# One attention and two-layer kernel: attention steps begun earlier, rounding split over two slots, all masks through ScalarE and GpSimd

## The chip, the core and the metric

The kernel runs on one core of a Trainium2 chip. The metric is the device time of one execution in microseconds (us), of which 0.2% (some 2 us) is about what a measurement of this kernel can tell from no change.

## What is computed

A gated linear attention over 768 positions, for 4 batches of 8 heads with head size 48, then two feed-forward layers over the 3072 resulting rows of 384 numbers:

```python
f = 1.0 / (1.0 + np.exp(-f_logit))
for t in range(S):
    state = f[:, :, t, :, None] * state + np.einsum('bhd,bhe->bhde', k[:, :, t], v[:, :, t])
    y[:, :, t] = np.einsum('bhd,bhde->bhe', q[:, :, t], state)
x = (x @ w_a) * (x @ w_b) @ w_out      # d_ff 1536
h = x @ w_in                           # d_ff 2048
out = (h - np.tanh(h)) @ w_out2
```

All inputs are float32. A product of two float32 matrices is made of three TensorE passes on rounded high halves and on low halves (`mm_split`: high by high, high by low, low by high), so each operand is first split: ScalarE copies it with rounding (the high half), then VectorE or GpSimd subtracts (the low half).

## The kernel before

**Attention steps.** Positions are cut in chunks of 64, and the four batches in two halves, which makes 24 steps; a step (`attn_step`, L289) handles one chunk of one half of the batches. It is a generator that yields between phases, and a phase has a letter:

- F: ScalarE's Sigmoid (L299). P: VectorE's scan PRE (L301). R: PMS, a reciprocal, and the reverse scan R (L304 to L306). K: VectorE's KH, RA and RB (L313 to L315). V: ScalarE copies the state into VS_A and VS_B (L318, L319).
- S: TensorE's scores sc from KH, RA and RB, and the transposes pk of KH (L327 to L331). M: the mask on sc, into RA and RB, and ScalarE's copy KTS of pk (L336 to L344). In steps 0 to 7 (`i < PSEL`) the mask is a ScalarE copy and a GpSimd select; from step 8 on VectorE multiplies by a tile of ones and zeros (L343).
- U: TensorE's uu from KTS, VectorE's T (L359), GpSimd's new state ST (L362). Y: TensorE's yy (L369). E: yy is split in high and low halves, of the tile y and of the tile x (ScalarE L383, VectorE L384). D: DMAs on ScalarE's and SyncE's queues move y into x (L390).

PSUM banks for sc, pk, the two uu and yy rotate: over two banks while block 0 runs, over three later (`att_bank`, `rot`).

**The first layer.** The rows of x are six blocks of 512, four steps each. `moe1` (L482) goes through block after block, and in each through 12 tiles m of d_ff. A tile has three parts, called slots here: nine matmuls a (then ScalarE's copy asb, L497), nine matmuls b (then VectorE's product gf, ScalarE's gh and the low half gl, L502 to L509), and nine matmuls y of the tile before (`y_group`). So a block has 36 slots. Steps 0 to 3 run ahead of everything, in the order of the string SEQ, in which x stands for a dummy matmul (warm) and c for one weight conversion; this is called the prologue. The steps of block j + 1 run in the slots of block j: phase p of its step si stands at slot 9 si + OFF[p] - LEAD of block j. Phases at negative slots fall into the block before, and for block 1 into SEQ.

**Weights.** The first layer's 36 weight tiles (w_a, w_b, w_o of each m) and the second layer's 32 come as compressed integers. A conversion (`w_tick`) is three VectorE instructions (L125 to L127, called a conversion below), a ScalarE copy w (L137) and a subtraction on GpSimd or, for the second layer, on VectorE (L139). In block 0 each slot makes one conversion of the first layer; in blocks 1 to 4 those of the second layer come at two slots of nine (`CONV`). Two conversions stand in SEQ, so in block 0 a conversion is made two ahead of the part that needs it.

At the start of blocks 1 to 5, in slot 2, the last y of the block before is finished, split by ScalarE (oh, L471) and VectorE (ol, L472) and written out (`store_x2`). The second layer comes after block 5, without attention.

Every engine works its instructions in the order in which this code emits them.

Of the kernel before, what the change touches and what calls it, by code (L numbers as in the profile page):

```python
# [9 lines left out]
F32 = mybir.dt.float32  # L10
# [3 lines left out]
ACTF = mybir.ActivationFunctionType  # L14
ALU = mybir.AluOpType
# [3 lines left out]
CH = 64  # L19
# [9 lines left out]
def tile_kernel(ctx: ExitStack, tc: tile.TileContext, q, k, v, f, w_a, w_b, w_out, w_in, w_out2, l_fkq, l_tv, l_v, l_w1, l_w2, out):  # L29
    nc = tc.nc  # L30
# [9 lines left out]
    U = 2 * NJ  # L40
# [8 lines left out]
    first = [sum(blocks[:j]) for j in range(NBLK)]  # L49
    block_of = [j for j, n in enumerate(blocks) for _ in range(n)]  # L50
    PRO = blocks[0]
    SLOTS = 3 * MF
    LEAD = 3
    PHASES = "FPRKVSMUYED"
    OFF = (0, 0, 1, 3, 4, 5, 5, 7, 8, 8, 9)
    CONV = (2, 6)
    PSEL = first[2]
    SEQ = ("lf0 lk0 lf1 lt0 lk1 lv0 lf2 lt1 lv1 lk2 w lf3 lt2 lv2 lk3 w lt3 lv3 w x x x x F0 P0 F1 R0 K0 x x lf4 lk4 x V0 S0 P1 M0 F2 "
           "R1 K1 U0 Y0 lt4 lv4 x V1 S1 P2 E0 F3 M1 R2 K2 x U1 Y1 x V2 S2 P3 E1 M2 R3 K3 x U2 Y2 x V3 S3 c E2 M3 c U3 x Y3 x F4 E3 P4")
    TW = 528  # L60

    const = ctx.enter_context(tc.tile_pool(name="const", bufs=1))
# [3 lines left out]
    stage = wctx.enter_context(tc.tile_pool(name="stage", bufs=2))  # L66

    ident = const.tile([128, 128], F32, name="ident")
    mask = const.tile([128, CH], F32, name="mask")
    D1 = const.tile([128, NS], F32, name="D1")  # L70
    PMS = const.tile([128, NSTEP, U], F32, name="PMS")
    okf = const.tile([1, 1], I32, name="okf")
# [70 lines left out]
    def w_spill():  # L143
        name, m, wt = spilled.pop(0)
        nc.sync.dma_start(out=wsp[2 * m + "ip".index(name)], in_=wt.bitcast(F32))
# [13 lines left out]
    def att_bank(name):  # L159
        rot["att"] = (rot["att"] + 1) % rot["n"]  # L160
        return bank(rot["att"], name)
# [5 lines left out]
    with tc.manual_schedule(), ExitStack() as p1:  # L167
# [81 lines left out]
        def load_v(i):  # L249
            w = w_of(i)  # L250
            for ab, (vs, r0) in enumerate(((w.VS_A, 64), (w.VS_B, 0))):
                nc.sync.dma_start(out=vs[r0:r0 + 64], in_=l_v[i, ab])
# [20 lines left out]
        for s_ in VX:  # L273
            for t in s_:
                nc.gpsimd.memset(t, 0.0)
        nc.gpsimd.memset(mask, 1.0)
        for r0 in (0, 64):
            nc.gpsimd.affine_select(
                out=mask[r0:r0 + 64], in_=mask[r0:r0 + 64], compare_op=ALU.is_ge, fill=0.0,
                base=0, pattern=[[1, CH]], channel_multiplier=-1,  # L280
            )

        X = {}
        Y3 = {}

# [3 lines left out]
        def attn_step(i):  # L289
            c, hb = divmod(i, 2)  # L290
# [34 lines left out]
            sc = att_bank("sc").rearrange("p (u s) -> p u s", s=CH)  # L325
# [6 lines left out]
                    pk[:, 128 * j:128 * (j + 1)], KH[:, 2 * j:2 * j + 2, :].rearrange("p u s -> p (u s)"), ident)  # L332
            yield
            for r_, rows in ((RA, slice(64, 128)), (RB, slice(0, 64))):
                if i < PSEL:
                    nc.scalar.activation(r_[rows], sc[rows], ACTF.Copy)  # L336
                    nc.gpsimd.affine_select(
                        out=r_[rows], in_=r_[rows], compare_op=ALU.is_ge, fill=0.0,
                        base=0, pattern=[[0, U], [1, CH]], channel_multiplier=-1,
                    )  # L340
                else:
                    m3 = mask.unsqueeze(1)
                    nc.vector.tensor_tensor(r_[rows], sc[rows], m3[rows].to_broadcast([64, U, CH]), ALU.mult)  # L343
            nc.scalar.activation(KTS, pk, ACTF.Copy)  # L344
            yield
            uus = [att_bank(f"uu{bl}").rearrange("p (u s) -> p u s", s=CH) for bl in range(2)]
# [32 lines left out]
            evac = [(xh[:, :, si], xl[:, :, si], yy[:, 0:U - 2].rearrange("p (j b) s -> p j (b s)", b=2))]  # L379
            if not direct:  # L380
                evac.insert(0, (Y3[jb][:, 0, si], Y3[jb][:, 1, si], yy[:, U - 2:U].rearrange("p b s -> p (b s)")))
            for dh, dl, src in evac:
                nc.scalar.activation(dh, src, ACTF.Copy)  # L383
                nc.vector.tensor_tensor(dl, src, dh.bitcast(F32), ALU.subtract)  # L384
            yield
            if si == ns - 1 and not direct:
                for kt in range(KT):
                    for hf, q_ in enumerate((nc.scalar, nc.sync)):
                        r, p0 = 64 * hf + 16 * kt, 48 + 64 * hf
                        q_.dma_start(  # L390
                            out=X[jb][p0:p0 + 16, :, kt, 0:ns].bitcast(F32),
                            in_=Y3[jb][r:r + 16, :, 0:ns].bitcast(F32))
# [9 lines left out]
        def flag(pr):  # L402
            nc.tensor.transpose(pr[0:1, 0:128], ru, ident)
            nc.vector.tensor_reduce(r2, pr[0:1, 0:128], mybir.AxisListType.X, ALU.min)
            nc.vector.tensor_scalar(okf, r2, 0.5, None, ALU.is_ge)

        gens = {i: attn_step(i) for i in range(NSTEP)}
        pulses = []
        for jb in range(1, NBLK):
            for si in range(blocks[jb]):  # L410
                for p, o in enumerate(OFF):
                    at = (9 * si + o) * SLOTS // (9 * blocks[jb]) - LEAD
                    pulses.append((SLOTS * (jb - 1) + at, first[jb] + si, p))
# [4 lines left out]
        def pulse(i, p):  # L418
            assert phase[i] == p
            phase[i] += 1  # L420
            if i >= PRO and p == 0 and i + 1 < NSTEP:
                load_t(i + 1, slice(0, 3))
                load_tv(i + 1)
            next(gens[i], None)
            if i >= PRO and PHASES[p] == "Y" and i + 1 < NSTEP:
                load_v(i + 1)
# [11 lines left out]
        def w_tick(upto):  # L438
            while nconv[0] < upto and (loaded or half):
                if loaded:  # L440
                    half.append(w_start(loaded.pop(0)))
                    w_fetch()
                if len(half) > 1 or not loaded or half[0][0] in "abo":
                    w_finish(half.pop(0))
                nconv[0] += 1
# [70 lines left out]
        for it in SEQ.split():  # L516
# [6 lines left out]
            elif it[0] == "l":  # L523
                i = int(it[2])
# [6 lines left out]
            else:  # L531
                i, p = int(it[1]), PHASES.index(it[0])
                if i >= PRO:
                    pulses.pop(0)
                pulse(i, p)
        for i in range(PRO):
            pulse(i, len(PHASES) - 1)
        npro = nconv[0]
# [13 lines left out]
        for g, jb in enumerate(moe1(None)):  # L552
# [3 lines left out]
            else:  # L556
                if g == SLOTS:
                    rot.update(n=3, conv=None)
                if spilled:
                    w_spill()  # L560
                if (g + LEAD) % (SLOTS // 4) in CONV and jb < NBLK - 1 or (jb == NBLK - 1 and slot == 0):
                    w_tick(min(nconv[0] + 1, NW2 + 1))
            while pulses and pulses[0][0] <= g:
                _, i, p = pulses.pop(0)
# [247 lines left out]
```

## Time and profile before

| what | value |
|---|---|
| median of 3 runs | 1009.82 us (1008.72 to 1010.71) |
| profiled execution, own time | 1008.59 us |
| its span | 1006.8 us |
| TensorE (PE) busy | 962.3 us, 96% of the span |
| VectorE (DVE) busy | 653.6 us, 65% |
| ScalarE (ACT) busy | 461.2 us, 46% |
| GpSimd (POOL) busy | 105.5 us, 10% |

The profiled execution's own time is 1.8 us over its span and 1.2 us under the median. The first a matmul starts at 39.3 us. Block 0 runs from there to about 158 us, blocks 1 to 4 to 528 us, block 5 to 603 us, the second layer to the end. A share of the whole span hides these stages, so the rows below are taken by stage.

### The profile page before, as it was taken

The numbers are of one execution on the slowest core, as the hardware profiler recorded it, in microseconds if no ns is written. First come the engines' busy times: TensorE is split into PE (matmuls) and PEld (weight loads), VectorE is DVE, ScalarE is ACT, GpSimd is POOL, SyncE is SP. The second block draws the span as 40 slices with busy tenths as digits, with TensorE's granted clock in tenths as the row PEclk, the third lists the DMA queues.
The fourth block names the chain that finished last, engine by engine and source line by source line (L and its number), as shares of the span: only waits on it lengthen the run. The fifth ranks groups of instructions, "written<-read, shape, count | busy, mean of one in ns | idle before, by whom it ended". The sixth has DMA issues, their size and how long they took to land.

```text
span 1006.8 us, 15823 instructions
## 1 busy us (share of the span) xinstructions
PE 962.3 (96%) x6151; PEld 769.9 (76%) x6151; DVE 653.6 (65%) x1077; ACT 461.2 (46%) x893; POOL 105.5 (10%) x115
## 2 busy tenths in 40 slices
PE   7788888999999999999999999999999999999997
PEld 4566666888788777878888888888888888888885
DVE  8788786666776676666663228666666666666663
ACT  4344442333333333333332127666666666666663
POOL 6455551000000000100000000000000000000000
PEclk9999998999999999999999999999999999999999
DMA  9365554444644453364428652010100100200000
GB/s 278 90 171 165 149 137 128 118 128 121 192 117 119 112 183 118 109 183 123 114 63 329 191 161 104 1 75 20 63 32 1 64 32 1 94 1 1 32 1 35
DMA packets 41170, 104.52 MB, mean 104 GB/s; under 512 B 5600, under 2 KB 8672, under 8 KB 41088
## 3 DMA queue, kind: packets, MB, share of 16 engines
q1 hardware_dynamic: 40368, 102.45, 34.0%
q10 hardware_dynamic: 720, 0.98, 0.5%
q8 instruction: 50, 0.82, 0.4%
q14 instruction: 32, 0.26, 0.1%
HBM read 74.71 MB, written 26.74 MB: 101 GB/s over the span
## 4 chain that ended last, share of the span: by engine, by line
PE 81%; DVE 11%; ACT 3%; issue 3%; DMA 2%; SPq 0%; POOL 0%; DVEq 0%; ACTq 0%
PE o L165 20%; PE h L165 20%; PE y L165 12%; PE a L165 12%; PE b L165 11%; PE yy L369 2%; DVE cv L126 2%; DVE cv L125 1%; DVE wc L127 1%; PE sc L327 1%; DVE R L306 1%; PE uu L351 1%; PE pk L331 1%; DMA x<-y 1%; DVE RB L315 1%
## 5 line engine op out<-in xcount | busy, mean ns | idle before, releaser
L165 PE MATMUL h<-x,w_i 128*128 128x512 f32 x864 | 213.0, 391 | 0.0
L165 PE MATMUL o<-gh,w_p 128*128 128x512 f32 x576 | 194.7, 393 | 0.0
L165 PEld LDWEIGHTS h<-x,w_i 128*128 128x128 f32 x864 | 162.2, 188 | 36.4
L165 PE MATMUL a<-x,w_a 128*128 128x512 f32 x648 | 166.1, 400 | 3.6 <-DMA x<-y 3.2
L165 PE MATMUL b<-x,w_b 128*128 128x512 f32 x648 | 163.4, 397 | 6.1 <-ACT w_b L137 5.0
L165 PE MATMUL y<-gh,w_o 128*128 128x512 f32 x432 | 151.1, 404 | 4.4 <-ACT w_o L137 3.3
L165 PEld LDWEIGHTS b<-x,w_b 128*128 128x128 f32 x648 | 123.2, 191 | 34.9 <-ACT w_b L137 6.3
L165 PEld LDWEIGHTS a<-x,w_a 128*128 128x128 f32 x648 | 118.6, 189 | 30.8 <-DMA x<-y 2.7
L105 DVE SCALAR_TENSOR_TENSOR xu<-u,h 128x512 f32<-128x512 f32 x96 | 66.0, 687 | 111.5 <-ACT u L102 111.3
L165 PEld LDWEIGHTS o<-gh,w_p 128*128 128x128 f32 x576 | 108.2, 188 | 24.7
L503 ACT ACTIVATE gh<-gf 128x512 fp32r<-128x512 f32 x72 | 45.5, 632 | 165.2 <-DVE gf L502 161.1
L102 ACT ACTIVATE u<-h 128x512 f32<-128x512 f32 x96 | 57.4, 598 | 132.8 <-PE h L165 132.1
L165 PE MATMUL o<-gl,w_p 128*128 128x512 f32 x288 | 113.1, 393 | 0.0
L165 PEld LDWEIGHTS y<-gh,w_o 128*128 128x128 f32 x432 | 82.0, 190 | 25.9 <-ACT w_o L137 4.9
L497 ACT ACTIVATE asb<-a 128x512 f32<-128x512 f32 x72 | 43.0, 597 | 100.0 <-PE a L165 99.4
L165 PE MATMUL y<-gl,w_o 128*128 128x512 f32 x216 | 85.8, 397 | 0.0
L502 DVE TENSOR_TENSOR gf<-asb,b 128x512 f32<-128x512 f32 x72 | 49.0, 681 | 54.2 <-PE b L165 49.6
L107 DVE SCALAR_TENSOR_TENSOR v<-v,v 128x512 f32<-128x512 f32 x96 | 66.5, 693 | 10.3 <-ACT gh L583 0.5
L106 DVE SCALAR_TENSOR_TENSOR v<-v,xu 128x512 f32<-128x512 f32 x96 | 66.5, 692 | 10.4 <-ACT v L103 0.5
L103 ACT ACTIVATE v<-u,bias 128x512 f32<-128x512 f32 x96 | 69.6, 725 | 3.1
L104 ACT ACTIVATE v<-u,bias 128x512 f32<-128x512 f32 x96 | 68.1, 710 | 0.7 <-DVE gl L584 0.7
L584 DVE TENSOR_TENSOR gl<-v,gh 128x512 fp32r<-128x512 f32 x96 | 65.8, 685 | 0.2 <-ACT gh L583 0.2
(100 smaller groups left out, 1105.1 us busy)
## 6 DMA issues: line engine op xcount, KB each, us to landing
wst<-in_l_w_dram SPq DMA_DIRECT2D x68, 384.0 KB, 3.3
wsp<-wst SPq DMA_DIRECT2D x32, 384.0 KB, 2.3
T<-in_l_fkq_dram SPq DMA_DIRECT2D x38, 288.0 KB, 5.1
x<-xs SPq DMA_DIRECT2D x12, 768.0 KB, 5.7
w_i<-wsp SPq DMA_DIRECT2D x16, 384.0 KB, 3.5
w_p<-wsp SPq DMA_DIRECT2D x16, 384.0 KB, 3.5
TV<-in_l_tv_dram SPq DMA_DIRECT2D x24, 192.0 KB, 5.1
xs<-oh SPq DMA_DIRECT2D x18, 256.0 KB, 2.2
```

What stands on the lines that cost most here:

```text
L102: nc.scalar.activation(u, h, ACTF.Square, accum_out=total)
L103: nc.scalar.activation(v1, u, ACTF.Square, bias=bias1)
L104: nc.scalar.activation(v2, u, ACTF.Square, bias=bias2)
L105: nc.vector.scalar_tensor_tensor(xu, u, Q4, h, ALU.mult, ALU.mult)
L106: nc.vector.scalar_tensor_tensor(v1, v1, Q_Y1, xu, ALU.add, ALU.mult)
L107: nc.vector.scalar_tensor_tensor(v2, v2, Q_Y2, v1, ALU.add, ALU.mult)
L126: nc.vector.scalar_tensor_tensor(t, hi, -1073741824, t, ALU.bitwise_and, ALU.bitwise_or)
L165: nc.tensor.matmul(dst, l_, r_, start=(first and i == 0), stop=(last and i == 2))
L497: nc.scalar.activation(asb, pb, ACTF.Copy)
L502: nc.vector.tensor_tensor(gf, asb, pab[1], ALU.mult)
L503: nc.scalar.activation(gh, gf, ACTF.Copy)
L584: nc.vector.tensor_tensor(gl, g, gh.bitcast(F32), ALU.subtract)
```

## The change

Five things change. The new phase L takes the VectorE half of E into a slot of its own: E now makes both ScalarE copies, L both subtractions. P gets a slot of its own after F; with both, the offsets of a step run from 0 to 11 instead of 0 to 9. LEAD is 6 instead of 3, so against before F stands three slots earlier, P to E two, the subtractions and D one; `CONV` follows. All steps mask with ScalarE's copy and GpSimd's select, and the tile of ones and zeros goes. SEQ has three conversions instead of two, three more dummy matmuls, and the phases R4, K4 and V4 of block 1's first step, which stood in block 0.

```diff
-    LEAD = 3
-    PHASES = "FPRKVSMUYED"
-    OFF = (0, 0, 1, 3, 4, 5, 5, 7, 8, 8, 9)
-    CONV = (2, 6)
-    PSEL = first[2]
+    LEAD = 6
+    PHASES = "FPRKVSMUYELD"
+    OFF = (0, 1, 2, 4, 5, 6, 6, 8, 9, 9, 10, 11)
+    CONV = (3, 7)
...
-           "R1 K1 U0 Y0 lt4 lv4 x V1 S1 P2 E0 F3 M1 R2 K2 x U1 Y1 x V2 S2 P3 E1 M2 R3 K3 x U2 Y2 x V3 S3 c E2 M3 c U3 x Y3 x F4 E3 P4")
+           "R1 K1 U0 Y0 lt4 lv4 x V1 S1 P2 E0 F3 M1 R2 L0 K2 x U1 Y1 x V2 S2 P3 E1 M2 L1 R3 K3 x U2 Y2 x V3 S3 x x E2 M3 c L2 F4 c P4 "
+           "x x U3 x Y3 x E3 L3 R4 c K4 V4")
...
-                if i < PSEL:
-                    nc.scalar.activation(r_[rows], sc[rows], ACTF.Copy)
-                    nc.gpsimd.affine_select(
-                        out=r_[rows], in_=r_[rows], compare_op=ALU.is_ge, fill=0.0,
-                        base=0, pattern=[[0, U], [1, CH]], channel_multiplier=-1,
-                    )
-                else:
-                    m3 = mask.unsqueeze(1)
-                    nc.vector.tensor_tensor(r_[rows], sc[rows], m3[rows].to_broadcast([64, U, CH]), ALU.mult)
+                nc.scalar.activation(r_[rows], sc[rows], ACTF.Copy)
+                nc.gpsimd.affine_select(
+                    out=r_[rows], in_=r_[rows], compare_op=ALU.is_ge, fill=0.0,
+                    base=0, pattern=[[0, U], [1, CH]], channel_multiplier=-1,
+                )
...
             for dh, dl, src in evac:
                 nc.scalar.activation(dh, src, ACTF.Copy)
+            yield
+            for dh, dl, src in evac:
                 nc.vector.tensor_tensor(dl, src, dh.bitcast(F32), ALU.subtract)
             yield
```

ScalarE at the end of the prologue: w_a and w_b are the copies of the first two conversions, x the high half of a step (E), RA, RB and KTS those of M3, F the Sigmoid of step 4, asb the first of block 0. Before:

```order
L137 ACTIVATE w_a_584<-wc 128x384
L383 ACTIVATE x<-yy 128x3x128
L336 ACTIVATE RA<-sc 64x512
L336 ACTIVATE RB<-sc 64x512
L344 ACTIVATE KTS<-pk 128x512
L137 ACTIVATE w_b_601<-wc 128x384
L299 ACTIVATE F<-T_181 128x8x64
L383 ACTIVATE x<-yy 128x3x128
L497 ACTIVATE asb<-a 128x512
```

And now:

```order
L371 ACTIVATE x<-yy 128x3x128
L327 ACTIVATE RA<-sc 64x512
L327 ACTIVATE RB<-sc 64x512
L332 ACTIVATE KTS<-pk 128x512
L136 ACTIVATE w_a_590<-wc 128x384
L291 ACTIVATE F<-T_180 128x8x64
L136 ACTIVATE w_b_605<-wc 128x384
L371 ACTIVATE x<-yy 128x3x128
L136 ACTIVATE w_a_675<-wc 128x384
L310 ACTIVATE VS_A<-ST_130 64x8x48
L311 ACTIVATE VS_B<-ST_130 64x8x48
L487 ACTIVATE asb<-a 128x512
```

M3's three copies now stand ahead of the copy of the first conversion instead of behind it.

VectorE in block 0, around the low halves of step 4 and the scan PRE of step 5 (cv and wc are a conversion, gf the product of a tile). Before:

```order
L127 SCALAR_TENSOR_TENSOR wc<-wst,cv 128x384
L384 TENSOR_TENSOR y_865<-yy,y_865 128x128
L384 TENSOR_TENSOR x<-yy,x 128x3x128
L125 TENSOR_SCALAR cv<-wst 128x384
L126 SCALAR_TENSOR_TENSOR cv<-wst,cv 128x384
L127 SCALAR_TENSOR_TENSOR wc<-wst,cv 128x384
L301 SCALAR_TENSOR_TENSOR PRE<-F,D_68 128x520
L502 TENSOR_TENSOR gf<-asb,b 128x512
```

And now:

```order
L126 SCALAR_TENSOR_TENSOR wc<-wst,cv 128x384
L374 TENSOR_TENSOR y_831<-yy,y_831 128x128
L374 TENSOR_TENSOR x<-yy,x 128x3x128
L293 SCALAR_TENSOR_TENSOR PRE<-F,D_67 128x520
L124 TENSOR_SCALAR cv<-wst 128x384
L125 SCALAR_TENSOR_TENSOR cv<-wst,cv 128x384
L126 SCALAR_TENSOR_TENSOR wc<-wst,cv 128x384
```

The subtractions and the scan now stand in one slot, one conversion behind the ScalarE copies y and x and the Sigmoid that they need.

ScalarE at the start of block 1, from the first asb on. Before:

```order
L497 ACTIVATE asb<-a 128x512
L503 ACTIVATE gh<-gf 128x512
L318 ACTIVATE VS_A<-ST_131 64x8x48
L319 ACTIVATE VS_B<-ST_131 64x8x48
L471 ACTIVATE oh<-y_823 128x512
L471 ACTIVATE oh<-y_824 128x512
L471 ACTIVATE oh<-y_825 128x512
L344 ACTIVATE KTS<-pk 128x512
```

And now:

```order
L487 ACTIVATE asb<-a 128x512
L327 ACTIVATE RA<-sc 64x512
L327 ACTIVATE RB<-sc 64x512
L332 ACTIVATE KTS<-pk 128x512
L493 ACTIVATE gh<-gf 128x512
L461 ACTIVATE oh<-y_867 128x512
L461 ACTIVATE oh<-y_868 128x512
L461 ACTIVATE oh<-y_869 128x512
```

KTS moves from behind the three copies oh of the block's end to ahead of them, and the two mask copies stand beside it; on VectorE the two mask products go.

## Rows read from the trace of the kernel before

**Rows 1.** Windows by stage: length; busy PE, PEld, DVE, ACT, POOL; clock; DMA; GB/s.
```profile
39.30:160.30 121.00, 101.14 (x725) 75.16 (x726) 99.48 (x166) 46.56 (x90) 60.73 (x58) 0.95 0.55 146
160.30:528.00 367.70, 361.40 (x2898) 289.86 (x2897) 246.28 (x439) 124.35 (x234) 21.61 (x16) 0.99 0.45 129
528.00:603.00 75.00, 75.00 (x329) 61.26 (x328) 20.23 (x31) 17.83 (x30) 0.00 (x0) 1.00 0.67 223
```

**Rows 2.** Timeline, end of the prologue: start, us, instruction [idle before <-releaser].
```profile
32.00 0.52 ACT L137 ACTIVATE w_a<-wc 128x384 fp32r<-128x384 f32 x1 [3.99 <-DVE wc L127]
32.93 0.59 ACT L336 ACTIVATE RA<-sc 64x512 f32<-64x512 f32 x1
...
34.67 0.27 PE L351 MATMUL uu<-TV,KTS 64*64 64x48 f32 x4 [3.21 <-ACT KTS L344]
...
39.31 0.50 PE L165 MATMUL a<-x,w_a 128*128 128x512 f32 x1 [0.26 <-ACT x L383]
```

**Rows 3.** Windows behind two long waits of PE, columns as in rows 1.
```profile
36.00:38.50 2.50, 2.50 (x48) 2.50 (x48) 0.14 (x1) 0.22 (x1) 1.65 (x2) 0.50 1.00 288
158.20:164.70 6.50, 6.03 (x14) 4.79 (x15) 3.10 (x4) 0.60 (x1) 0.86 (x1) 0.50 0.02 4
```

**Rows 4.** Timeline of DVE: K's last instruction in steps 4, 5 and 7.
```profile
46.20 0.69 DVE L315 TENSOR_TENSOR RB<-T,PRE 64x512 f32<-64x512 f32 x1
...
75.10 1.39 DVE L315 TENSOR_TENSOR RB<-T,PRE 64x512 f32<-64x512 f32 x1
...
134.62 1.39 DVE L315 TENSOR_TENSOR RB<-T,PRE 64x512 f32<-64x512 f32 x1
```

**Rows 5.** Waits of DVE, 40 to 158 us: us in total, times, longest.
```profile
DVE PRE L301 <- ACT F L299: 6.4, 4, 2.9
...
DVE y L384 <- ACT y L383: 3.0, 4, 0.8
DVE x L384 <- ACT x L383: 2.2, 4, 0.6
```

**Rows 6.** Timeline of DVE, block 0: two conversions' starts, P, and R.
```profile
47.53 0.56 DVE L125 TENSOR_SCALAR cv<-wst 128x384 int32<-128x384 int32 x1
...
49.37 0.56 DVE L125 TENSOR_SCALAR cv<-wst 128x384 int32<-128x384 int32 x1
...
93.37 1.57 DVE L301 TENSOR_TENSOR_SCAN PRE<-F,D 128x520 f32<-128x520 f32 x1 [1.18 <-ACT F L299]
...
97.08 0.55 DVE L304 TENSOR_SCALAR PMS<-PRE 128x8 f32<-128x8 f32 x1
...
97.90 2.00 DVE L306 TENSOR_TENSOR_SCAN R<-F,D 128x520 f32<-128x520 f32 x1
```

**Rows 7.** Timeline, ACT's queue, SP's queue and PE, from block 0 into block 1.
```profile
151.81 0.71 ACTq L390 DMA_DIRECT2D x<-y  x1
...
152.09 0.58 SPq L247 DMA_DIRECT2D T<-in_l_fkq_dram  x1
...
154.96 0.93 PE L165 MATMUL a<-x,w_a 128*128 128x512 f32 x3 [1.39 <-DMA x<-y]
158.67 1.65 PE L165 MATMUL a<-x,w_a 128*128 128x512 f32 x3 [0.53 <-DMA x<-y]
160.12 4.04 PE L165 MATMUL b<-x,w_b 128*128 128x512 f32 x9
```

**Rows 8.** Waits of PE, 160 to 604 us: us in total, times, longest.
```profile
PE uu L351 <- DVE RB L343: 4.6, 3, 1.5
PE uu L351 <- ACT KTS L344: 1.0, 3, 0.4
PE sc L328 <- DVE RB L315: 0.7, 3, 0.3
```

**Rows 9.** Groups by shape: count, busy us, mean ns: VectorE's mask, GpSimd's select.
```profile
L343 DVE TENSOR_TENSOR RA<-sc,mask 64x512 f32<-64x512 f32 x16 | 11.1, 695 | 1.9 <-PE sc L328 0.9
...
L337 POOL TENSOR_SCALAR_AFFINE_SELECT RB<-RB 64x512 f32<-64x512 f32 x8 | 6.7, 838 | 0.5
```

More of the change, by code (lines that the diff above doesn't have):

```diff
@@ L68, in tile_kernel @@
     ident = const.tile([128, 128], F32, name="ident")
-    mask = const.tile([128, CH], F32, name="mask")
     D1 = const.tile([128, NS], F32, name="D1")
@@ L275, in tile_kernel @@
                 nc.gpsimd.memset(t, 0.0)
-        nc.gpsimd.memset(mask, 1.0)
-        for r0 in (0, 64):
-            nc.gpsimd.affine_select(
-                out=mask[r0:r0 + 64], in_=mask[r0:r0 + 64], compare_op=ALU.is_ge, fill=0.0,
-                base=0, pattern=[[1, CH]], channel_multiplier=-1,
-            )
         X = {}
@@ L334, in attn_step @@
             for r_, rows in ((RA, slice(64, 128)), (RB, slice(0, 64))):
-                if i < PSEL:
-                    nc.scalar.activation(r_[rows], sc[rows], ACTF.Copy)
-                    nc.gpsimd.affine_select(
-                        out=r_[rows], in_=r_[rows], compare_op=ALU.is_ge, fill=0.0,
-                        base=0, pattern=[[0, U], [1, CH]], channel_multiplier=-1,
-                    )
-                else:
-                    m3 = mask.unsqueeze(1)
-                    nc.vector.tensor_tensor(r_[rows], sc[rows], m3[rows].to_broadcast([64, U, CH]), ALU.mult)
+                nc.scalar.activation(r_[rows], sc[rows], ACTF.Copy)
[3 more added lines that the diff above has]
+                )
             nc.scalar.activation(KTS, pk, ACTF.Copy)
```

## The prediction

> **What bounds the kernel now.** I read the windows by stage first [rows 1]. The reader is to see that TensorE is full in block 5 and behind it, nearly full in blocks 1 to 4 (6.3 us idle in 367.7), and not in block 0, where it idles 19.9 of 121.0 us while VectorE works 99.5. So nothing can be won behind 528 us, little in blocks 1 to 4, and most in the prologue and block 0. Block 5 has no attention and takes 75.0 us, or 2.08 us a slot; blocks 1 to 4 take (367.7 - 6.3) / 4 = 90.4, so the TensorE work of one attention step is (90.4 - 75.0) / 4 = 3.8 us. Block 0 with 36 slots and four steps would be about 90 us of TensorE; it takes some 119. The waits of TensorE behind 160 us [rows 8] give the 6.3 us: one and the same hitch at three block starts.
>
> Within block 0 the rhythm is nine slots to a step. RB, the last instruction of K, ends at 46.89, 76.49 and 136.01 us in steps 4, 5 and 7 [rows 4]: 29.7 us a step, against 9 x 2.08 + 3.8 = 22.5 us of TensorE. VectorE sets this rhythm. It also waits: on ScalarE's Sigmoid before P and on ScalarE's copies before each low half [rows 5].
>
> **The prologue.** ScalarE works in order, and M3 stands behind the copy w_a, which waited 3.99 us for a conversion and ran at 32.00; M3's first copy began at 32.93 [rows 2]. TensorE had been idle 3.21 us when uu began at 34.67, so sc and the transposes were done at 31.46, and sc about 0.6 earlier. With M3 ahead of w_a its copies can begin near 30.9, 2.0 us earlier. Behind that wait yy ran at the 1.2 GHz level (granted clock 0.50 from 36.0 to 38.5 us [rows 3]); without it I take it at the full clock, which saves half of some 2.5 us, so 1.2. E3 and the first a matmul then come 3.2 to 3.4 us earlier, at about 36.0 instead of 39.31. The third conversion and K4 cannot delay this, since they stand behind L3 on VectorE. The second conversion and P4 lie ahead of U3's additions there, but yy needs only the masks.
>
> From L3 (36.0 to 36.6) VectorE has R4, a conversion and K4: 1.7 + 1.85 + 2.2 us, so K4 ends at 42.4 instead of 46.9. A conversion is 1.85 us from one start to the next [rows 6].
>
> **Block 0.** The waits on the Sigmoid and on the two copies are 6.4 + 3.0 + 2.2 us [rows 5]; the longest of the first, 2.9, lies behind the last conversion. The new L and P remove all of it, 8.7 us up to there or 2.2 to 2.9 us a step. But this is not what block 0 gains, because the new order puts a tighter ring in place of the slack. In a step of the change TensorE's sc waits for K on VectorE, and only behind sc come b, y, uu, a, yy and the next b; the product gf of that b stands on VectorE ahead of the next L, P, R and K. The ring is:
> - TensorE, from K's end to the end of the second b: 3.8 + 4 x 2.08 = 12.1 us. VectorE has about 10.5 us of its own meanwhile (five conversions, a gf, T), so it idles some 1.6 us.
> - VectorE from that gf to the end of the next K: two gf 1.2, four conversions 7.4, the low halves 0.85 (0.29 and 0.56), P 1.57, R with its two short instructions 2.8, K 2.7 (RB took 1.39 where GpSimd ran beside it and 0.69 where not [rows 4]): 16.5 us.
>
> Together 28.6 us, against 29.7 now. TensorE idles about 6 us of each round in one piece, just ahead of sc. Both long waits shown, before uu in the prologue and before block 1, have a stretch at clock 0.50 behind them [rows 3], and in the change such a stretch would lie on the ring's TensorE part and add up to 1.5 us. So a round is 28.6 to 30.1 us; I take 29.2. K7 ends at 42.4 + 3 x 29.2 = 130.0 us, six earlier than now.
>
> After K7 TensorE has sc to yy of step 7 and eight slots (three b, two a, three y): 3.8 + 8 x 2.08 = 20.4, with some half clock 21.2, so it is through block 0 at about 151.2. VectorE: gf of tile 10 at 130 + 12.9 = 142.9, then a conversion, the low halves, P, and the last conversion: 0.6 + 1.85 + 0.85 + 1.57 + 1.85 = 6.7, so 149.6, and ScalarE's w_o 150.2. Only then does ScalarE issue D, which it works in order behind that copy, as now at 151.81 [rows 7]. Now the three parts of x land late: the a matmuls that need them begin at 154.96 and, for the last third, 158.67, while SyncE began the T loads at 152.09 in their midst. In the change the Sigmoid phase that issues those loads stands two slots ahead of D. I take 3.1 us from the first issue to the first part, as now, and 0.65 us for each further one: a ends near 155.3, against 160.3. The stretch at clock 0.50 from 158.2 to 164.7 [rows 3], in which b took 4.04 us instead of 2.08, should mostly go: 2.5 us more. By the start of block 1 the gain is 5.0 + 2.5 = 7.5 us.
>
> **Blocks 1 to 4.** At three block starts S stood in slot 2, behind the three copies oh and the three subtractions ol, so KTS and the VectorE mask came late and uu waited. Now S and M stand in slot 0, ahead of them; U's additions come behind ol, but nothing on TensorE needs them before the next step. All of 4.6 + 1.0 + 0.7 = 6.3 us goes [rows 8]. The masks: 32 VectorE products of 0.70 us are replaced by 32 ScalarE copies of 0.59 and 32 selects of 0.69 to 0.84 [rows 2, 9]. VectorE loses 22 us of 246, ScalarE gains 19 on 124, GpSimd some 25 on 22, none near the stage's 367.7 [rows 1], so I cost it at nothing. What hides it: between sc and uu TensorE has b and y, 4.2 us, and three ScalarE copies in a row are 1.8; between sc and yy it has some 7, and the selects end about 2.5 us after sc. If this cover is gone, uu or yy waits in each of 16 steps.
>
> The price beside that is contention. The row shows RB stretched from 0.69 to 1.39 us when GpSimd ran beside it [rows 4]. The Trainium skill ("SBUF — State Buffer", Who interferes with whom) says that a VectorE instruction with two SBUF inputs and a GpSimd one that reads SBUF share a port that one holds to its end, which speaks against selects on GpSimd; the trace agrees, as RB doubled. By that rule all 32 selects could hold VectorE for their length, 32 x 0.77 = 25 us. VectorE has 121 us free in this stage, so this moves the end only as part of the last rival below.
>
> **The sum.** 7.5 + 6.3 = 13.8 us off the profiled execution's 1008.6 (span 1006.8 and 1.8 around): 994.8. The median of the runs is 1.2 over that execution, so I say 995.
>
> **The rivals.**
> - *VectorE alone sets block 0.* The ring does not bind because TensorE gets ahead, and each step loses the whole wait: rounds of 26.5 to 27 us. K7 ends at 42.4 + 3 x 26.7 = 122.5, a of block 1 near 148 instead of 155.3. For it: VectorE is the busiest by far in block 0. Against it: sc cannot start before K. Time 1008.6 - 21 = 987.5.
> - *Half clock and new waits eat block 0.* Rounds of 30 us or more, D's landing again 5 to 7 us behind its issue, another half-clock stretch at the start of block 1. Then 0 to 2 us remain there and the 6.3 of the block starts: 1000 to 1002.
> - *Slower: the mask's new chain is not covered.* In blocks 1 to 4 uu needs KTS behind two more ScalarE copies, yy needs two selects, and each select can hold VectorE as RB was held [rows 4]. If each of 16 steps pays the 1.9 us that uu paid at three block starts (6.3 with sc's share, over three) the bill is 30 us, and the block starts lose nothing of theirs: 1008.6 - 7.5 + 30 = 1031. It decides from 0.5 us a step on, where 16 x 0.5 eats the 7.5. Against it: steps 4 to 7 use this chain already, and TensorE was then late by VectorE and not by a select.
>
> **How the numbers follow.** Forecast 60%, the first rival 17%, the second 15%, the slower one 6%, the rest of 2% no change. Sizes within the forecast run from 991 to 999. 8 in 10 reach from the first rival's time to the second's: 986.5 to 1002. Faster by over 0.2% (about what a measurement of this kernel can tell from no change): 0.91; within 0.2%: 0.03; slower: 0.06.
>
> **What would show it.** The first a matmul near 36 us, with uu in the prologue waiting under 1.5 us and no clock of 0.50 ahead of it. In block 0 no wait of PRE, y or x on ScalarE; instead sc waiting 4 to 6 us for RB once a step, and RB's ends 28.6 to 30.1 us apart. The first wait of block 1's a on x under 2 us in sum. No PE wait on uu at the starts of blocks 2 to 4, and 361 to 363 us for blocks 1 to 4. I am wrong if RB's ends are closer than 28 us, if TensorE waits for KTS or a select in ordinary steps of blocks 1 to 4, or if the first a is no earlier than 38 us.

## The result and the profile after

The changed kernel takes 998.17 us, the median of four runs (996.94 to 1000.26), against 1009.54 for the kernel before beside it. The ratio is 0.989, with a 95% interval from 0.987 to 0.991. The forecast was 995.0 with a range of 986.5 to 1002, so sign and range held and the time lay 3.2 us above it. The profiled execution of the changed kernel took 997.97 us (span 996.3), 10.6 less than the one before.

The windows by stage (columns as in [rows 1]) show block 0 with the prologue's tail, blocks 1 to 4, and block 5:

```profile
35.00:155.50 120.50, 100.32 (x715) 79.50 (x715) 93.72 (x164) 47.07 (x91) 66.26 (x59) 0.89 0.58 153
155.50:517.20 361.70, 361.65 (x2905) 289.93 (x2906) 218.06 (x408) 137.55 (x266) 35.89 (x49) 1.00 0.47 131
517.20:591.60 74.40, 74.40 (x325) 60.77 (x325) 19.54 (x29) 17.71 (x30) 0.00 (x0) 1.00 0.65 218
```

TensorE has no idle time left in blocks 1 to 4. The granted clock of block 0 fell from 0.95 to 0.89. The lengths of its two windows can't be set side by side, since that of [rows 1] ends at block 1's first b and this one at its first a: from first a to first a the block takes 120.6 us where it took 115.6. The starts of matmul groups, taken from both traces, split the 10.6 us (10.5 of the span):

| stretch | before | after | gain |
|---|---|---|---|
| start to first a | 39.31 | 34.97 | 4.3 |
| first a to second a of block 1 | 128.73 | 130.80 | -2.1 |
| from there to second a of block 5 | 363.99 | 355.62 | 8.4 |
| from there to the end of the span | 474.8 | 474.9 | -0.1 |

The first uu of block 1's attention moved ahead of the second a, so 0.6 us belongs to the second row instead of the third.

**Prologue.** The timeline that answers [rows 2] (ScalarE's mask copy, uu, the first a):

```profile
29.81 0.59 ACT L327 ACTIVATE RA<-sc 64x512 f32<-64x512 f32 x1 [0.92 <-PE sc L320]
...
31.79 0.68 PE L339 MATMUL uu<-TV,KTS 64*64 64x48 f32 x32
...
34.97 2.70 PE L164 MATMUL a<-x,w_a 128*128 128x512 f32 x9 [0.26 <-ACT x L371]
```

Of uu's wait of 3.21 us 0.64 us is left, and the clock between 31 and 36 us is 1.00. The change also has four more dummy matmuls in SEQ, not three, and all four run here, from 30.19 to 31.86 us, where TensorE would have waited. The run e3 below moves M3 without them.

**Block 0.** The waits of VectorE from 35 to 155 us, which answer [rows 5]:

```profile
DVE gf L492 <- PE b L164: 13.2, 5, 4.6
DVE gf L492 <- POOL RA L328: 5.4, 2, 2.7
DVE gf L492 <- POOL w_b L138: 1.8, 1, 1.8
DVE gf L492 <- ACT asb L487: 1.2, 1, 1.2
DVE x L374 <- ACT x L371: 0.3, 1, 0.3
```

Before, VectorE waited for ScalarE ahead of PRE, y and x. Those waits have all but gone, and ahead of gf it waits 21.6 us where it had waited 4.0, nearly all for TensorE's b. (Where the releaser reads POOL RA or w_b, b ended last too: at 78.89 us b had just finished, as the fences of the round from 72 to 102 us show.) K's last instruction in steps 4 to 7, which answers [rows 4]:

```profile
40.17 1.37 DVE L307 TENSOR_TENSOR RB<-T,PRE 64x512 f32<-64x512 f32 x1
...
71.87 0.69 DVE L307 TENSOR_TENSOR RB<-T,PRE 64x512 f32<-64x512 f32 x1
...
101.26 0.69 DVE L307 TENSOR_TENSOR RB<-T,PRE 64x512 f32<-64x512 f32 x1
...
129.72 0.69 DVE L307 TENSOR_TENSOR RB<-T,PRE 64x512 f32<-64x512 f32 x1
```

It ends at 41.5, 72.6, 101.9 and 130.4 us: rounds of 31.0, 29.4 and 28.5. One round, from 72 to 102 us, TensorE first and then VectorE:

```profile
71.98 0.44 PE L319 MATMUL sc<-RA,KH 64*64 64x64 f32 x2 [3.93 <-DVE RA L306]
...
75.27 3.49 PE L164 MATMUL b<-x,w_b 128*128 128x512 f32 x9
...
84.74 2.34 PE L164 MATMUL b<-x,w_b 128*128 128x512 f32 x9
```

```profile
78.89 0.69 DVE L492 TENSOR_TENSOR gf<-asb,b 128x512 f32<-128x512 f32 x1 [2.64 <-POOL RA L328]
...
87.21 0.69 DVE L492 TENSOR_TENSOR gf<-asb,b 128x512 f32<-128x512 f32 x1 [1.80 <-PE b L164]
...
89.54 0.28 DVE L374 TENSOR_TENSOR y<-yy,y 128x128 fp32r<-128x128 f32 x1
89.75 0.55 DVE L374 TENSOR_TENSOR x<-yy,x 128x384 fp32r<-128x384 f32 x1
90.21 1.23 DVE L293 TENSOR_TENSOR_SCAN PRE<-F,D 128x520 f32<-128x520 f32 x1
...
93.44 1.24 DVE L298 TENSOR_TENSOR_SCAN R<-F,D 128x520 f32<-128x520 f32 x1
...
99.75 1.47 DVE L306 TENSOR_TENSOR RA<-T,PRE 64x512 f32<-64x512 f32 x1
```

This is the ring of the prediction. TensorE waits 3.93 us for K ahead of sc, then its first b takes 3.49 us where the second takes 2.34, so gf waits 2.64 and again 1.80 us, and behind the second gf stand L, P, R and K. The clock behind three of TensorE's waits, in windows:

```profile
40.20:56.20 16.00, 13.19 (x124) 10.59 (x125) 9.09 (x16) 6.79 (x14) 8.24 (x9) 0.71 0.38 104
74.50:78.80 4.30, 4.30 (x15) 3.63 (x15) 1.62 (x3) 4.19 (x8) 2.57 (x3) 0.62 0.61 179
155.50:161.00 5.50, 5.45 (x46) 4.23 (x47) 1.85 (x2) 1.60 (x4) 1.33 (x1) 0.69 0.01 3
```

**Block 0 into block 1**, which answers [rows 7]: ScalarE's last w_o, D behind it, and block 1's first a.

```profile
151.01 0.53 ACT L136 ACTIVATE w_o<-wc 128x384 fp32r<-128x384 f32 x1 [2.93 <-DVE wc L126]
151.07 1.99 ACTq L380 DMA_DIRECT2D x<-y  x3
...
155.55 3.54 PE L164 MATMUL a<-x,w_a 128*128 128x512 f32 x9 [2.29 <-DMA x<-y]
```

### The profile page after: what moved, and what is told of

It is laid out like the page before. It is cut to its first block, busy times and chain, and to the rows that moved or that the text cites. A ratio compares the mean times of both kernels' runs of the same rounds, so it can differ in the third digit from the quotient of the medians.

```text
span 996.3 us, 15895 instructions
## 1 busy us (share of the span) xinstructions
PE 961.1 (96%) x6155; PEld 773.3 (78%) x6155; DVE 620.4 (62%) x1045; ACT 475.1 (48%) x925; POOL 123.3 (12%) x144
## 4 chain that ended last, share of the span: by engine, by line
PE 89%; DVE 7%; issue 1%; DMA 1%; ACT 1%; POOL 0%; DVEq 0%; ACTq 0%
PE o L164 20%; PE h L164 20%; PE b L164 15%; PE a L164 13%; PE y L164 13%; PE yy L357 2%; PE sc L319 2%; PE pk L323 1%; PE uu L339 1%; DVE cv L125 1%; PE sc L320 1%; DVE cv L124 1%; DVE PRE L293 1%; DVE RA L306 1%; DVE R L298 1%
## 5 line engine op out<-in xcount | busy, mean ns | idle before, releaser
L164 PE MATMUL b<-x,w_b 128*128 128x512 f32 x648 | 169.3, 407 | 0.0
L164 PE MATMUL y<-gh,w_o 128*128 128x512 f32 x432 | 146.1, 393 | 0.0
L493 ACT ACTIVATE gh<-gf 128x512 fp32r<-128x512 f32 x72 | 45.6, 633 | 125.9 <-DVE gf L492 125.7
```

Of the source, the lines that this page charges most:

```text
L164: nc.tensor.matmul(dst, l_, r_, start=(first and i == 0), stop=(last and i == 2))
L493: nc.scalar.activation(gh, gf, ACTF.Copy)
```

## Experiments

Each was timed beside the kernel before. A round is the time from one end of RB, the last instruction of K, to the next, in block 0. Two theories stood against each other from the start. One says that block 0 gives the gain back because the clock falls to half behind TensorE's wait ahead of sc. The rival says that VectorE's own work sets the round whatever the clock does. Later runs take the end of block 0, the other edits one by one, and the number of conversions in the prologue.

**The clock taken out: e4_fill.** Dummy matmuls fill TensorE's wait ahead of S. They go into the PSUM bank of b, which b needs again only behind sc.

```diff
+            if jb == 0 and slot % 9 == 0:
+                t = bank(4, "warm")
+                for _ in range(17):
+                    nc.tensor.matmul(t, wdum[:, 0:128], wdum, start=True, stop=True)
```

> The changed kernel plus 17 dummy matmuls ahead of sc in each of block 0's four steps, where TensorE now waits 4 us for K; nothing is left out. Theory R (a ring from K on VectorE over sc, y and two b on TensorE back to gf and K on VectorE sets block 0, and the half clock behind the wait lies on it): no clock of 0.50 behind these waits, RB's ends 26.5 to 28 us apart instead of 28.5 to 31.0, time 989 to 993 us. Rival V (VectorE's own instructions set the pace): rounds as they are, 997 to 999 us.

Measured: 988.0 us (987.5 to 992.4), ratio 0.982 [0.979, 0.986]: 10 us under the changed kernel, though TensorE does four groups of 3.84 us more. The window of block 0, and TensorE's waits ahead of sc from 38 to 150 us:

```profile
35.00:147.50 112.50, 105.46 (x800) 77.46 (x795) 94.36 (x167) 46.84 (x92) 66.92 (x60) 1.00 0.63 165
```

```profile
PE sc L320 <- DVE RB L307: 1.0, 3, 0.3
PE sc L319 <- DVE RA L306: 0.8, 3, 0.3
```

The clock is 1.00 and RB's ends lie 27.0, 27.5 and 27.4 us apart. The three rounds make 81.9 us against 88.9 in the changed kernel, so half clock costs 6 to 7 us there. A price for each round can't be read from this: e1 and e8 below, which have the same order of work up to K7, take 29.8, 28.6 and 29.7, so single rounds differ by over 1 us from trace to trace, and the sum by 0.8. The first a of block 1 waited 2.12 us for x, nearly as long as in the changed kernel (2.29), and ran in 2.30 us instead of 3.54.

**The split undone: e2_unsplit.** P goes back to F's slot and L to E's.

```diff
-    OFF = (0, 1, 2, 4, 5, 6, 6, 8, 9, 9, 10, 11)
+    OFF = (0, 0, 2, 4, 5, 6, 6, 8, 9, 9, 9, 11)
```

> The changed kernel with P back in F's slot and the low halves L back in E's slot; slots of F, R, K, S, U, Y and D and the masks stay. Theory R: VectorE's part of the ring gets back the waits on ScalarE, 2 to 2.9 us a round, so 1004 to 1008 us. Rival (VectorE has slack in the ring and takes them in it): 997 to 999 us.

Measured: 993.7 us (992.6 to 996.1), ratio 0.987 [0.985, 0.989]. I had not expected that: without the split the kernel is 4.5 us faster. VectorE from 83 to 88 us:

```profile
85.02 0.29 DVE L374 TENSOR_TENSOR y<-yy,y 128x128 fp32r<-128x128 f32 x1 [1.14 <-ACT x L371]
85.23 0.55 DVE L374 TENSOR_TENSOR x<-yy,x 128x384 fp32r<-128x384 f32 x1
85.69 1.23 DVE L293 TENSOR_TENSOR_SCAN PRE<-F,D 128x520 f32<-128x520 f32 x1
86.84 0.67 DVE L492 TENSOR_TENSOR gf<-asb,b 128x512 f32<-128x512 f32 x1
```

The wait for ScalarE is back (1.14 us), but L and P now stand ahead of gf, and gf no longer waits. In the changed kernel VectorE waits 1.80 us for b at that place and does L and P (1.8 us from 89.54 to 91.36) behind it, on the part of the ring that K's end hangs on. The split took a wait of ScalarE away and moved work out of another wait. L and P were moved together here, so what each is worth alone is not shown.

**D one slot earlier: e8_d10.**

```diff
-    OFF = (0, 1, 2, 4, 5, 6, 6, 8, 9, 9, 10, 11)
+    OFF = (0, 1, 2, 4, 5, 6, 6, 8, 9, 9, 10, 10)
```

> The changed kernel with D in L's slot, one slot earlier, so that ScalarE issues its part of D ahead of the last conversion's copy. My theory: block 1's first a no longer waits 2.3 us for x, and the half clock behind that wait goes: 994 to 996 us. Rival (the DMAs of D are slow for other traffic and land as late): 997 to 999 us.

Measured: 994.1 us (993.3 to 994.6), ratio 0.985 [0.982, 0.987]. ScalarE's D and the first a of block 1:

```profile
147.85 2.01 ACTq L380 DMA_DIRECT2D x<-y  x3
...
152.69 2.22 PE L164 MATMUL a<-x,w_a 128*128 128x512 f32 x9
```

D no longer stands behind the copy w_o of the last conversion, a waits for nothing and runs at full clock. This place cost the changed kernel 4 us.

**The masks: e1_oldmask.** Steps 8 to 23 multiply on VectorE again.

```diff
+                if i < PSEL:
                     nc.scalar.activation(r_[rows], sc[rows], ACTF.Copy)
...
+                else:
+                    m3 = mask.unsqueeze(1)
+                    nc.vector.tensor_tensor(r_[rows], sc[rows], m3[rows].to_broadcast([64, U, CH]), ALU.mult)
```

> The changed kernel with the masks of steps 8 to 23 back on VectorE; nothing else. My theory: the hitch of uu at the block starts went because S and M stand ahead of the copies oh, so nothing comes back: 997 to 999 us, blocks 1 to 4 within 0.5 us. Rival M (the hitch went because VectorE no longer masks): TensorE waits again for RB and KTS at three block starts, 1003 to 1005 us.

Measured: 998.8 us (997.6 to 999.5), ratio 0.992 [0.990, 0.994]. The intervals of the two ratios overlap and blocks 1 to 4 take the same 355.6 us, with no wait of TensorE in either. The masks on GpSimd are worth nothing by themselves, and they cost nothing.

**The lead: e6_lead4 and e10_shift.** The first is the changed kernel with steps begun four slots ahead instead of six, the second the kernel before with five instead of three and nothing else changed.

```diff
-    LEAD = 6
+    LEAD = 4
...
-           "x x U3 x Y3 x E3 L3 R4 c K4 V4")
+           "x x U3 x Y3 x E3 L3 R4 c")
```

> The changed kernel with LEAD 4, so that S and M stand in slot 2 of a block again, behind oh and ol; K4 and V4 leave the prologue for slots 0 and 1 of block 0. My theory: the hitches come back, with all masks on ScalarE behind oh, 2 us or more at each of three block starts, and D again comes late: 1004 to 1010 us. Rival M (the VectorE mask made the hitch): blocks 1 to 4 as in the changed kernel, 997 to 1001 us.

Measured: 1007.1 us (1005.0 to 1011.0, ten runs), ratio 0.999 [0.997, 1.001]: nothing is left of the gain. TensorE from 38 to 160 us, then from 150 to 600 us:

```profile
PE sc L319 <- DVE RA L306: 7.8, 4, 2.2
PE sc L320 <- DVE RB L307: 4.1, 4, 1.1
PE a L164 <- DMA x<-y: 4.0, 1, 4.0
```

```profile
PE a L164 <- DMA x<-y: 10.0, 3, 3.6
...
PE uu L339 <- ACT KTS L332: 0.6, 1, 0.6
```

The size was as I had expected, the cause only in part. The hitch ahead of uu came once, with 0.6 us. What eats the gain is that D, at offset 11, now stands in the last slot but one of each block, so that the first a of blocks 1 to 4 waits for x, 14.0 us in all. From second a of block 1 to that of block 5 the run takes 373.1 us, over 17 more than the changed kernel. In block 0 it is faster: RB ends at 43.8, 71.1, 98.4 and 125.7 us, three rounds of 27.3, and from first a to second a of block 1 it takes 122.7 us instead of 130.8, with three conversions ahead and with the split. S now stands behind a y and not behind an a, and L and P stand between two gf, of which the later one does not wait: VectorE waits once a round for b, 1.5 us at most, and TensorE ahead of sc 3.0 us (7.8 + 4.1 over four steps). So what the split and the third conversion cost, as told in e2 and e11, holds for the slots of LEAD 6. The rounds of LEAD 4 with D moved up were not run.

```diff
-    LEAD = 3
+    LEAD = 5
...
-           "... F4 E3 P4")
+           "... F4 E3 P4 R4 K4 V4")
```

> The kernel before with LEAD 5 alone: every phase two slots earlier, R4, K4 and V4 in the prologue; no new slots, VectorE's masks and two conversions in the prologue stay. My theory: S stands in slot 0, so the hitches at three block starts go (6 to 8 us), D stands in slot 31 and block 1 does not wait for x (2 to 4 us); block 0's rounds stay at 29 to 30 us: 996 to 1001 us. Rival (the split and the ScalarE masks carry the gain): 1004 to 1008 us.

Measured: 1004.5 us (1003.4 to 1005.5), ratio 0.995 [0.993, 0.996], in the rival's range, though e1 and e2 speak against its cause. TensorE from 160 to 600 us:

```profile
PE sc L327 <- DVE RA L314: 2.0, 4, 0.5
PE sc L328 <- DVE RB L315: 1.3, 4, 0.3
```

No wait of uu is left, so the earlier steps alone remove the hitch of [rows 8]. But with P in F's slot and D at offset 9, D of one step stands in the same slot as F of the next one, ahead of it on ScalarE, and sc waits 0.8 us for K at the starts of blocks 2 to 4 and once inside block 3. That the one causes the other was not tried. In block 0 there are 10.7 us of waits of y for w_o, on ScalarE's copy and GpSimd's subtraction. From second a of block 1 to that of block 5 the run takes 360.6 us, against 364.0 before and 355.6 in the changed kernel. So the shift alone gives part of the gain of blocks 1 to 4, and some 5 us in all.

**The prologue: e3_m3first.** The kernel before with M3 ahead of the conversion.

```diff
-           "... V3 S3 c E2 M3 c U3 x Y3 x F4 E3 P4")
+           "... V3 S3 E2 M3 c c U3 x Y3 x F4 E3 P4")
```

> The kernel before with one thing of the change: in the prologue M3 and E2 stand ahead of both conversions. My theory: the first a matmul starts near 36 us instead of 39.3, and all of it reaches the end: 1004.5 to 1006 us where before is 1008 to 1009. Rival (VectorE sets block 0 whatever the first a does): under 1 us, 1007.5 to 1009.

Measured: 1006.9 us (1002.2 to 1008.4, ten runs), ratio 0.997 [0.996, 0.999]. The first a comes at 36.14 us, 3.2 earlier, the size that the prediction gave to this edit, but only about 2 us of it reach the end (1.8 by the medians), between the two expectations. RB ends at 43.75 and 74.99 us, 3.1 and 1.5 earlier than before: the round between takes 31.2 us instead of 29.6. Behind its first wait ahead of sc, of 2.2 us, the clock is 0.50 (43 to 46 us), where behind the same wait in the kernel before, 2.15 us, it is 1.00.

**One conversion fewer in the prologue: e11_two_conv.** The changed kernel with its third conversion left to block 0.

```diff
-           "x x U3 x Y3 x E3 L3 R4 c K4 V4")
+           "x x U3 x Y3 x E3 L3 R4 K4 V4")
```

> The changed kernel with two conversions in the prologue instead of three, as before the change. My theory: with weights only two ahead, y waits for w_o in block 0 as in the run with LEAD 5 alone (some 2.5 us a round), against K4 1.85 us earlier: 1000 to 1004 us where the changed kernel has 998. Rival (the third conversion only moves 1.85 us of VectorE about): 996 to 999 us.

Measured: 987.5 us (987.1 to 989.1), ratio 0.979 [0.976, 0.981]. Neither theory had that: I expected a loss, and it is as large a gain as that of the dummies. TensorE's waits over one round, and block 0's window:

```profile
56.67 1.89 PE L164 MATMUL b<-x,w_b 128*128 128x512 f32 x7 [0.67 <-POOL w_b L138]
...
59.91 0.73 PE L164 MATMUL y<-gh,w_o 128*128 128x512 f32 x2 [0.88 <-POOL w_o L138]
...
62.48 1.88 PE L164 MATMUL a<-x,w_a 128*128 128x512 f32 x7 [0.24 <-POOL w_a L138]
...
65.77 0.30 PE L319 MATMUL sc<-RA,KH 64*64 64x64 f32 x2 [1.41 <-DVE RA L306]
66.39 0.27 PE L320 MATMUL sc<-RB,KH 64*64 64x64 f32 x1 [0.33 <-DVE RB L307]
```

```profile
35.00:145.30 110.30, 94.39 (x716) 71.41 (x716) 92.36 (x163) 45.92 (x90) 64.68 (x58) 0.98 0.61 163
```

TensorE idles 3.5 us in this round (0.67 + 0.88 + 0.24 + 1.41 + 0.33), hardly less than the 4.1 of the changed kernel, but in pieces, each ahead of a weight just made or of sc, and the clock of block 0 is 0.98 instead of 0.89. With a third conversion ahead, in the slots of LEAD 6, a, b and y never wait for weights; TensorE runs on and waits ahead of sc in one piece, with half clock behind it. By K's ends (39.3, 66.3, 95.0 and 122.5 us) the run is 2.2 us ahead at step 4, since the conversion no longer stands ahead of K4, and 7.9 us at step 7. It is 10.3 ahead at the first a of block 1, which no longer waits for x. One stretch at half clock is left (a b of 3.61 us at 68.18).

**Put together.** e12_unsplit_d10 has P at 0, L at 9 and D at 10; e9_best adds the dummies of e4; e13_two_unsplit_d10 is e12 with two conversions, and e14_two_best has the dummies as well. All four have

```diff
-    OFF = (0, 1, 2, 4, 5, 6, 6, 8, 9, 9, 10, 11)
+    OFF = (0, 0, 2, 4, 5, 6, 6, 8, 9, 9, 9, 10)
```

> The changed kernel with P in F's slot, the low halves in E's slot and D one slot behind them; no dummies. My theory: the two gains add, 993.7 less the 4.1 us that D one slot earlier gave: 989 to 991 us. Rival (both remove the same wait at the start of block 1): 992 to 994.5 us.

> The changed kernel with the 17 dummy matmuls ahead of sc in block 0, P in F's slot, the low halves in E's slot and D one slot behind them. My theory: 2 to 4 us under the run with the dummies alone (988.0): 984 to 986 us. Rival (with the clock kept up, TensorE sets block 0 and P's and L's place is worth nothing): 986 to 989 us.

> The changed kernel with two conversions in SEQ instead of three, P back in F's slot and L in E's, and D at offset 10. Alone the conversion gave 10.7 us and the other two together 7.1 us. Theory 'one cause' (both gains come from the same thing, a round of block 0 in which TensorE waits in one long piece ahead of sc with the half clock behind it): without that piece the offsets have only D's 2 us left to give, so 985 to 988, block 0's RB ends 26.5 to 27.5 us apart, granted clock of the whole above 0.99. Theory 'two causes' (the split lengthens VectorE's part of the round whatever TensorE's wait looks like): the gains add, 979 to 983, rounds below 26 us.

> The same with 17 dummy matmuls ahead of S in slots 0, 9, 18 and 27 of block 0. With three conversions the dummies gave 10 us and this set 983.7. Where only two conversions run ahead, TensorE has no long wait ahead of sc into which dummies (3.7 us each group at full clock) fit: theory 'short waits keep the clock' says they gain nothing and cost part of their 15 us in all, so 986 to 995, at or over the run without them. Rival: a half-clock stretch is left in some round and the dummies still take it away, then 980 to 984, under the run without them.

| run | us (lowest to highest) | ratio | rounds of RB |
|---|---|---|---|
| e12_unsplit_d10 | 991.1 (990.0 to 992.3) | 0.982 [0.979, 0.984] | 29.4, 28.0, 27.8 |
| e9_best | 983.7 (982.5 to 984.2) | 0.974 [0.972, 0.977] | 26.4, 26.5, 26.5 |
| e13_two_unsplit_d10 | 987.9 (985.8 to 988.7) | 0.978 [0.975, 0.982] | 26.4, 28.0, 26.5 |
| e14_two_best | 990.1 (989.5 to 991.5) | 0.981 [0.978, 0.984] | 28.3, 28.1, 28.0 |

With three conversions the gains of the offsets and of D's place add for the most part (4.5 and 4.1 apart, 7.1 together), and with the dummies the kernel is 14.4 us under the changed one: the fastest of all. TensorE is then busy for 104.4 of block 0's 107.9 us (35.0 to 142.9 us), 15 of them with dummies. With two conversions the offsets give nothing (987.9 against 987.5), as "one cause" expected: where TensorE does not wait in one long piece there is little left for them to repair. The dummies seem to cost there (990.1 against 987.9, with overlapping intervals), since no long wait takes them in, though the clock is 1.00 with them; that is what "short waits keep the clock" expected for the time. It does not hold of every short wait. The windows of e13 behind sc's waits in steps 5, 6 and 7:

```profile
66.50:72.00 5.50, 5.11 (x44) 4.57 (x45) 3.98 (x7) 2.91 (x6) 1.29 (x2) 0.69 0.31 77
94.50:100.00 5.50, 5.15 (x51) 4.36 (x52) 4.79 (x9) 2.94 (x6) 1.32 (x2) 1.00 0.30 80
121.00:126.50 5.50, 5.12 (x44) 4.50 (x45) 3.97 (x7) 2.92 (x6) 1.29 (x2) 0.69 0.32 79
```

Ahead of all three sc waits 1.4 us for RA and 0.3 for RB, and the clock behind is 0.69, 1.00 and 0.69. The first of them lies in e13's round of 28.0 us, the second in one of 26.5.

## Why the prediction was right, and where it was off

**First a: right, 1 us short.** M3 ahead of the copy w_a removes uu's wait and the half clock behind it, as worked out: e3 alone, without the dummies, has 1.2 us of that wait left, full clock behind it, and gives the 3.2 us of that step. The first a came at 34.97 instead of 36.0. The six other runs with the same string SEQ (e1, e2, e4, e8, e9, e12) have it at 35.64 to 36.65, so the extra 1 us is mostly this one trace's.

**The round of block 0: right in sum by luck, wrong in both parts.** The prediction gave TensorE 12.1 us from K's end to the second b and VectorE 16.5 from there to the next K, 28.6 in all, and took 29.2; K7 was to end at 130.0 and ended at 130.4. From 72.56 to gf at 87.21 are 14.65 us, 2.5 more than the first part, because sc, pk and b ran at half clock. The 1.5 us that I allowed at most were too few. From 87.21 to 101.95 are 14.7 us, 1.8 less than the second part. From start to start R with its two short instructions takes 1.6 us for 2.8, P 1.15 for 1.57, the four conversions 6.8 for 7.4, and K 3.3 for 2.7. In [rows 6] R and P had 2.00 and 1.57 us, begun while GpSimd worked; here they begin first and take 1.24 and 1.23, while RA, begun while GpSimd works, takes 1.47. I had carried the stretched durations over. Two errors of opposite sign left the sum standing. e4 shows the first alone: at full clock TensorE's part, from 69.59 to the end of the second b at 82.2, is 12.6 us. Of the signs named, the first round lies outside (31.0 for 28.6 to 30.1), and TensorE waits 4.1 us in one piece and not about 6.

**What the split is worth: wrong in sign.** The text credited L and P with 2.2 to 2.9 us of waits a step and then said that a tighter ring takes it back. Its ring held L and P on VectorE's part without asking what happens if they stay ahead of gf, in the 1.6 us in which it let VectorE idle. e2 answers: with both ahead of gf the kernel is 4.5 us faster.

**The third conversion: costed at nothing, and it costs 10.7 us.** The prediction only asked whether it delays the prologue. It does not delay the first a, but K4 ends 2.2 us later with it. It also lengthens the weights' lead, so TensorE waits in one piece, and e11 without it is 10.7 us faster. With S in other slots the lead need not cost that: e6 has it and rounds of 27.3 us. "TensorE idles about 6 us of each round in one piece" was in the text as a fact of the ring; that the piece can be cut up was not.

**The end of block 0: mechanism right, size off by 5.2 us.** Of 7.5 us expected by the start of block 1, 2.3 came. K7 held. The last conversion ended at 150.97 for 149.6 and w_o at 151.54 for 150.2, which is 1.3 us. D's first part was to land 3.1 us behind its issue; a began 4.5 us behind ScalarE's issue at 151.07, and its wait was 2.29 us where the text had set under 2 as a sign. The two rows of the DMA table, median times from issue to landing over the whole program, before and after:

```profile
x<-y SPq DMA_DIRECT2D x15, 64.0 KB, 2.6
x<-y ACTq DMA_DIRECT2D x15, 64.0 KB, 2.5
```

```profile
x<-y SPq DMA_DIRECT2D x15, 64.0 KB, 4.1
x<-y ACTq DMA_DIRECT2D x15, 64.0 KB, 4.2
```

These medians are of five block ends. At this one ScalarE's three transfers took 3.0, 4.6 and 5.4 us before and 4.3, 3.9 and 3.7 after, SyncE's 2.4 to 2.5 before and 4.5, 4.0 and 3.2 after. Of ScalarE's parts the first, with whose landing at 155.42 us a begins, took 1.3 us longer; I had taken its time of before as it stood. And the half clock that was "mostly to go" stayed: behind a's wait of 2.29 us the window shows 0.69. D, which the change put one slot behind L, is the step at fault: e8 moves it up, issues it 3.2 us earlier, has it landed within 2.5 to 3.2 us, and gains 4.1 us. This is the second rival's mechanism (half clock and new waits, D's landing late), at a price of 5.2 us where the rival had 5.5 to 7.5.

**Blocks 1 to 4: right, 1.5 us more.** The waits on uu and sc are gone, 6.3 us as forecast. Over blocks 2 to 4 the stretch from first a to first a fell from 276.2 to 268.5 us, of which 6.3 us were idle time of TensorE [rows 8] and 1.4 its busy time (269.9 to 268.5), which I have not traced to an instruction. e1, with VectorE's masks, has the same 355.6 us as the changed kernel, so the earlier start does this and not the masks.

**The rivals.** VectorE alone setting block 0 fell: rounds of 26.4 to 26.5 throughout came only with dummies and without the split. The slower one fell too. uu and yy never waited for a select in blocks 1 to 4. Of contention the traces show RA at 1.47 us where a GpSimd subtraction had begun before it and at 0.68 where none ran, which agrees with the rule of the Trainium skill ("SBUF — State Buffer", Who interferes with whom) that the prediction named. Which of the two is stretched goes by which begins first: where the scan R began at 93.44 and the subtraction of w_a at 93.72, R kept its 1.24 us and the subtraction took 1.78 instead of 1.0. But e1, in which GpSimd works 13.9 us in the stage instead of 35.9, is no faster: where VectorE has 140 us free the rule has no price.

## What to carry over

In a ring between two engines, a wait that is removed by moving work past another wait can lengthen the ring: list for each instruction on which side of the engine's remaining wait it will stand, and move it only towards that wait. Idle time of TensorE can have a second price, the clock behind it. In block 0 here 4.1 us of a round in one piece went with a clock of 0.89, and 3.5 us in pieces with 0.98; but single waits of one length came out either way, so read the clock behind each wait from the trace. Where one long wait stands ahead of an attention step or a block start, either fill it, cut it up by letting other operands arrive just in time, or remove it. A prepared lead (weights made earlier) is worth nothing in itself when it only collects short waits into a long one. And before an order is given up, try its steps a slot or two earlier or later: with LEAD 4 the same steps made block 0 faster by 8 us and lost more than that at the block starts.

## What the runs showed of the hardware

- One wait of 3.9 us ahead of sc was followed by a stretch at about half clock in each round (b 3.5 us instead of 2.2 to 2.3), a cost of some 10 us up to the second a of block 1. Some 3.5 us a round in pieces of 0.2 to 1.4 us left the clock of block 0 at 0.98.
- The length of a wait alone did not decide it. Behind sc's waits of 1.4 and 0.3 us in e13 the clock was 0.69 twice and 1.00 once; behind waits of block starts for x in e6 it was 0.51 after 3.0 us (242.8 to 249.0 us) and 1.00 after 3.3 us (339.1 to 345.4 us). What else decides it is not shown.
- Dummy matmuls of 3.84 us in that wait gained 10 us where it existed, and none where it did not.
- The same 64 KB transfers took 2.5 us from issue to landing before and 4.2 after in the median, in e4 and e8 too (4.1 to 4.5). At the last of the five block ends, where no further attention step is loaded, they took 2.3 to 2.9 us in all these runs; at the earlier ones 2.3 to 5.4 before and 3.2 to 5.2 after. What the slow ones share their time with was not separated.
- VectorE's scan R took 2.00 us where a GpSimd subtraction had begun just before it (at 97.80 us, R at 97.90), and 1.24 where R began first or ran alone; the product RA took 1.47 and 0.68. Where VectorE had begun first, the subtraction took 1.8 to 2.0 us instead of 1.0.
